# Attention, then two expert layers: 576-query score units in PSUM pairs, one product bank, a tied TensorE order

## The chip, the cores and the metric

One core of one Trainium2 chip. The metric is the device time of one execution in microseconds. The engines are named as in the profile: PE (TensorE, with PEld for its weight loads), DVE (VectorE), ACT (ScalarE), POOL (GpSimd) and SP (SyncE, which here only issues DMAs).

## The reference

```
q_pool = q.reshape(B, H, S // 2, 2, D).mean(axis=3)           # B, H, S, D = 4, 8, 1152, 64
scores = scale * q_pool @ k^T                                 # 576 x 1152 for each of 32 heads
attn   = exp(scores - max); attn /= sum(attn) + 1e-9
x      = attn @ v                                             # heads side by side: 2304 x 512
x      = moe(x)        # top-1 of 8 experts, 512 -> 1024 -> 512, times the gate
out    = (h * cos(h)) @ w_out,  h = x @ w_in                  # 512 -> 2048 -> 512
```

All inputs are float32. The kernel keeps float32 accuracy by splitting operands into a high and a low part (fp32r for scores, f16 for weights and values) and adding the products.

## The kernel before

The program has three stages: attention (32 heads, the first 616 us of the profiled execution), the experts, and the cosine layer. The change touches attention alone, and the DMAs that fill `y_d` with zeros while attention runs.

For each head i, in this order:

- `load` (L111 to L123) fetches k, q, v. The q pairs are added, k and q are split (ACT `q_high`, `k_high`; DVE or POOL `q_low`, `k_low`), transposed on PE into PSUM tiles `pk`, `pq`, copied out by ACT as `k1`, `q1`, and rearranged in SBUF by DMAs (`k2`, `q2`). `v` is scaled by a power of two and split into `va` (high by POOL L177, low by DVE L182).
- `scores` and `row_max` (L247, L262): PE makes 128 x 384 score tiles `pm`; DVE reduces each to row maxima `mm`. 12 tiles for an odd head, 15 for an even head, which does the last 64 queries of its odd neighbour along with its own. `max_all` (L268) reduces them to `mx`, and `max_row` (L277) has SP write the negated maxima into a row of `q2` by small DMAs (4 for a head, 2 more for the shared rest).
- `weight_scores` (L287, L288): the scores again, transposed (128 keys by queries), with the maximum subtracted by the extra row of `q2`. Nine groups c of 128 keys, each in two halves j of 288 queries; a half `pst` takes one of three PSUM banks. `weight_exp` (L296): ACT takes the exponential of each half into the SBUF tile `pf`, 128 x 576.
- `weight_high` and `weight_low` (L308 to L318): `ph` is `pf` cast to f16, `pl` the rest. The nine casts are spread as 6 on ACT, 1 on DVE and 2 on POOL, the nine subtractions as 2 on DVE (c = 4 and 7) and 7 on POOL.
- `values` (L335 to L337): for each of five query tiles a run of 27 matmuls (9 groups by three products) into a PSUM bank of its own, `po`; ACT copies it to `pe` (L341). `normalise` (L359 to L362) on DVE divides by the row sums and writes the head's columns of `xf` and `xs`.

The heads are software-pipelined: while PE makes weight scores of head i it also makes maxima of head i+1, products of head i-1, and transposes of heads i+2 and later. The order comes from `plan`: each step is given a time from the table `G` in units where a head takes T = 12.8; steps are issued sorted by that time, and a scheduler that simulates the program then orders each engine's instructions, so that two steps that are near in the plan may change places or interleave. PSUM has 8 banks: 3 for `pst` (pool `ps2`), 3 for `pm` and small things (`psm`), 2 for `pk`, `pq` and `po` (`ps1`).

`Routing.plan` adds, after each batch of 8 heads, transposes of x, gate logits, ranks, and on POOL 4 or 5 indirect DMAs (`scatter`, L483). `Routing.zeros` (L505 to L510) makes SP issue 18 DMAs of 256 KB of zeros into `y_d`, all at one place of the plan, after head 2.

Of the kernel before, what the change touches and what calls it, by code (L numbers as in the profile page):

```python
# [8 lines left out]
F32 = mybir.dt.float32  # L9
# [20 lines left out]
    kh=3.8, kl=5.8, qp=4.5, qh=5.3, ql=6.3, vm=5.15, va=6.0, vs=8.0, vh=10.3,  # L30
    vl=10.5, qt=1.05, qc=0.6, q2=0.9, q1=2.95, k0=2.25, kg=1.7, kc=0.05, kd=1.7,
    o0=0.1, mo=0.78, m=0.8, mr=0.3, ma=0.0, md=0.4, w=3.35, e=1.7, h=0.8,
    l=0.55, v=3.2, vc=2.8, vt=0.3, vx=0.3, n=1.1,
)
HI_ACT = (0, 2, 4, 5, 6, 8)
HI_DVE = (3,)
LO_DVE = (4, 7)
K_COPY_DVE = ()
QEARLY = (2, 3)
# [4 lines left out]
class Attention:  # L44
# [15 lines left out]
    def __init__(self, tc, ctx, pools, q, k, v, ident, xpool):  # L60
# [12 lines left out]
        self.k2, self.q1, self.q2, self.va, self.mm, self.qr, self.pe = [], [], [], [], [], [], []  # L73
# [7 lines left out]
        const(self.pe, (cp,) * 2, "pe", [5, 66])  # L81
# [25 lines left out]
    def set_pe(self, i):  # L107
        self.nc.gpsimd.memset(self.pe[i], 1.0)


    def load(self, i):  # L111
        nc = self.nc
        b, h = divmod(i, H)
        s = self.st[i] = {}
        qr = self.qr[i % 2]
        s["kr"] = kr = self.p1.tile([P, NK, D], F32, tag="kr", name=f"kr_{i}")
        s["vr"] = vr = self.p1.tile([P, NK, D], F32, tag="vr", name=f"vr_{i}")
# [5 lines left out]
        nc.sync.dma_start(vr, self.v[b, h].rearrange("(p c) d -> p c d", p=P))  # L123
# [12 lines left out]
    def q_low(self, i):  # L136
        s = self.st[i]
        eng = self.nc.gpsimd if i in QEARLY else self.nc.vector
# [47 lines left out]
    def k_transpose(self, i, g):  # L186
        nc, s = self.nc, self.st[i]
        ps = s["pk", g] = self.ps1.tile([P, 512], F32R, tag="ps1", name=f"pk_{i}_{g}")
# [3 lines left out]
    def k_copy(self, i, g):  # L192
# [4 lines left out]
        if g in K_COPY_DVE:  # L197
            nc.vector.tensor_copy(o, s["pk", g][:, :384])
        else:
            nc.scalar.copy(o, s["pk", g][:, :384])  # L200
# [11 lines left out]
    def q_transpose(self, i, part):  # L212
        nc, s = self.nc, self.st[i]
        pool, tag = ((self.ps1, "ps1"), (self.psm, "psm"))[part]
# [32 lines left out]
    def scores(self, i, ci, g):  # L247
        nc = self.nc
        ps = self.st[i]["pm", ci, g] = self.psm.tile([P, 512], F32, tag="psm", name=f"pm_{i}_{ci}_{g}")
        ks = slice(g * 384, (g + 1) * 384)  # L250
        if ci < 4:
            q0 = self.q_cols(i, 0)[0].start + ci * P
            nc.tensor.matmul(  # L253
                ps[:, :384], self.st[i]["q1"][:, q0 : q0 + P], self.st[i]["k1"][:, ks], start=True, stop=True
            )
            return
        for h in (i, i + 1):
            q = self.q1[h % 4][:, 512:] if h == i else self.q1[h % 4][:, :P]
# [11 lines left out]
    def max_row(self, i, part):  # L270
        mx = self.mx[i % 4].bitcast(F32)
        for h, o, c in [(i, 0, c) for c in range(4)] if part == 0 else [(i, 0, 4), (i + 1, 64, 4)]:
# [4 lines left out]
            self.nc.sync.dma_start(row, mx[o : o + n, c : c + 1])  # L277


    def weight_scores(self, i, c, j):  # L280
        nc, s = self.nc, self.st[i]
        if (c, j) == (0, 0):
            s["ph"] = self.pw.tile([P, NK, SQ], F16, tag="ph", name=f"ph_{i}")
            s["pl"] = self.pw.tile([P, NK, SQ], F16, tag="pl", name=f"pl_{i}")
        ps = s["pst", c, j] = self.ps2.tile([P, 512], F32, tag="ps2", name=f"pst_{i}_{c}_{j}")
        ks, o = slice(c * P, (c + 1) * P), slice(j * 288, (j + 1) * 288)
        nc.tensor.matmul(ps[:, :288], s["k1"][:, ks], s["q1"][:, o], start=True, stop=False)  # L287
        nc.tensor.matmul(  # L288
            ps[:, :288], self.k2[i % 3][: D + 2, ks], self.q2[i % 4][: D + 2, o], start=False, stop=True
        )  # L290

    def weight_exp(self, i, c, j):
        nc, s = self.nc, self.st[i]
        if j == 0:
            s["pf", c] = self.p3.tile([P, SQ], F32, tag="pf", name=f"pf_{i}_{c}", bufs=4)
        nc.scalar.activation(  # L296
            s["pf", c][:, j * 288 : (j + 1) * 288], s["pst", c, j][:, :288], AF.Exp, scale=0.0625
        )

    def weight_high(self, i, c):  # L300
        nc, s = self.nc, self.st[i]
        ph, pf = s["ph"][:, c, :], s["pf", c]
        if i == B * H - 1:
            hi_act, hi_dve = (0, 2, 4, 6, 8), (1, 3, 5, 7)
        else:
            hi_act, hi_dve = HI_ACT, HI_DVE
        if c in hi_act:
            nc.scalar.copy(ph, pf)  # L308
        elif c in hi_dve:
            nc.vector.tensor_copy(ph, pf)  # L310
        else:
            nc.gpsimd.tensor_scalar(ph, pf, 1.0, 0.0, op0=ALU.mult, op1=ALU.add)

    def weight_low(self, i, c):
        nc, s = self.nc, self.st[i]
        lo_dve = (0, 2, 3, 5, 6, 8) if i == B * H - 1 else LO_DVE
        eng = nc.vector if c in lo_dve else nc.gpsimd
        low = eng.tensor_sub(s["pl"][:, c, :], s["pf", c], s["ph"][:, c, :])  # L318
        if c not in lo_dve:
            self.low = getattr(low, "ins", low)  # L320
# [5 lines left out]
    def values(self, i, ci, third):  # L326
# [3 lines left out]
        if third == 0:  # L330
            s["po", ci] = self.ps1.tile([P, 512], F32, tag="ps1", name=f"po_{i}_{ci}")
        po, va = s["po", ci][self.rows(i, ci), :], s["va"]
        for c in range(3 * third, 3 * third + 3):
# [12 lines left out]
    def normalise(self, i):  # L346
# [8 lines left out]
        pe = self.pe[i % 2]  # L355
# [3 lines left out]
        nc.vector.tensor_scalar(r, pe[:, :, D], PSC * 1e-9, s["iv"], op0=ALU.add, op1=ALU.mult)  # L359
        nc.vector.reciprocal(r, r)  # L360
        nc.vector.tensor_mul(full[:, :, cols], pe[:, :4, :D], r[:, :4].unsqueeze(2).to_broadcast([P, 4, D]))
        nc.vector.tensor_scalar_mul(self.xs[b // 2 * 9 + 4][half, cols], pe[half, 4, :D], r[half, 4:5])  # L362

    def plan(self, at, n=B * H):

        for t, f, m in (
            (-1.95, self.set_qr, 2), (-0.9, self.set_q, 4), (-0.3, self.set_q2, 4), (0.0, self.set_k, 3),
            (0.3, self.set_v, 5), (1.0, self.set_pe, 2),
# [3 lines left out]
        for i in range(n):  # L372
# [34 lines left out]
            for c in range(NK):  # L407
                z9 = w + c * T / NK
                for j in range(2):
                    a(z9 + T / 18 * j, self.weight_scores, c, j)  # L410
                    a(z9 + T / 18 * j + G["e"], self.weight_exp, c, j)
                a(z9 + T / 18 + G["e"] + G["h"], self.weight_high, c)
                a(z9 + T / 18 + G["e"] + G["h"] + G["l"], self.weight_low, c)
# [1023 lines left out]
```

## Time and profile before

| | |
|---|---|
| three runs, us | 1355.69, 1356.85, 1363.11 (median 1356.85) |
| the profiled execution | 1359.03 us; its span, first to last instruction, 1357.4 us |
| granted TensorE clock, mean over the span | 0.957 |
| busy share of the span | PE 91%, DVE 75%, ACT 54%, POOL 48% |
| attention, first exponential to last | 39.4 us to 609.8 us |

The profile is of one execution. "Busy" of an engine is the time covered by its instructions. PE's matmuls overlap (a product matmul lasts 0.19 us, and the next starts 0.03 us after it), so its busy time is more than the time that it needs; the distance from one start to the next says what a matmul costs. A clock of 1.00 is 2.4 GHz and 0.50 is 1.2 GHz.

### The profile page before, as it was taken

Reading aid. Unit: us, or ns where it says so; the run is one execution under the profiler, and the core shown is the slowest. Engines: PE = TensorE matmul, PEld = TensorE weight load, DVE = VectorE, ACT = ScalarE, POOL = GpSimd, SP = SyncE. Lnnn points to the kernel's source line nnn. Section 1 sums busy time; section 2 is a strip of 40 time slices with the busy share of each in tenths; the row PEclk is TensorE's granted clock in tenths of the full one; section 3 lists DMA queues with packets and bytes.
Section 4 is the critical chain, followed back from the end, with each engine's and each line's share of the span. In section 5 each row is a group of like instructions: output and inputs, shape, how many; then the busy total and the mean of one; then the engine's idle time right before and its main releaser. Section 6 shows DMA issues by size and latency. Waiting matters only on the chain. (4 is left out here: it accounts for less than half of the span.)

```text
span 1357.4 us, 26889 instructions
## 1 busy us (share of the span) xinstructions
PE 1237.3 (91%) x10190; PEld 1049.8 (77%) x10190; DVE 1021.3 (75%) x1921; ACT 728.0 (54%) x1631; POOL 654.9 (48%) x585
## 2 busy tenths in 40 slices
PE   5897999999889997999699898987998999999996
PEld 4786887888778786878588788866887888888885
DVE  6896888997879878886368788977765667667664
ACT  4685886788758775882265555664322223222232
POOL 6796888798779877751244435526002002010010
PEclk8798998999989998999799999999999999999998
DMA  8349344343433332324588879975002001000000
GB/s 182 88 111 191 83 98 87 100 102 82 108 80 89 81 99 47 99 64 91 119 248 300 258 239 288 318 245 186 1 0 65 1 0 63 0 32 15 0 32 16
DMA packets 117691, 146.20 MB, mean 108 GB/s; under 512 B 34864, under 2 KB 73904, under 8 KB 117552
## 3 DMA queue, kind: packets, MB, share of 16 engines
q1 hardware_dynamic: 104176, 114.97, 32.0%
q0 software_dynamic: 5600, 15.25, 3.6%
q10 hardware_dynamic: 7776, 14.17, 3.2%
q8 instruction: 82, 1.34, 0.5%
q14 instruction: 57, 0.47, 0.1%
HBM read 97.57 MB, written 28.43 MB: 93 GB/s over the span
## 5 line engine op out<-in xcount | busy, mean ns | idle before, releaser
L318 POOL TENSOR_TENSOR pl<-pf,ph 128x576 f16<-128x576 f32 x220 | 306.1, 1404 | 54.8 <-ACT ph L308 38.0
L262 DVE TENSOR_REDUCE mm<-pm 128x1 f32<-128x384 f32 x432 | 224.7, 546 | 54.4 <-PE pm L253 40.0
L296 ACT ACTIVATE pf<-pst 128x288 f32<-128x288 f32 x576 | 222.1, 421 | 81.1 <-PE pst L288 52.6
L287 PE MATMUL pst<-q,k 128*128 128x288 f32 x576 | 199.1, 351 | 1.8 <-ACT pf L296 1.6
L483 POOL DMA_INDIRECT out_dram<-os,token x18 | 18.2, 1013 | 354.5 <-ACT os L1200 186.9
L288 PE MATMUL pst<-q,k 66*128 66x288 f32 x576 | 173.9, 308 | 14.9 <-DMA q<-mx 14.9
L337 PE MATMUL po<-va,pl 128*128 128x66 f16 (+1 forms) x1440 | 176.8, 198 | 6.3 <-DVE pl L318 5.1
L335 PE MATMUL po<-va,ph 128*128 128x66 f16 (+1 forms) x1440 | 176.1, 198 | 0.3 <-ACT pe L341 0.3
L336 PE MATMUL po<-va,ph 128*128 128x64 f16 (+1 forms) x1440 | 175.1, 196 | 0.0
L1171 ACT ACTIVATE a<-a,hpi 128x512 f32<-128x512 f32 (+1 forms) x80 | 54.5, 681 | 201.9 <-DVE a L1170 192.3
L253 PE MATMUL pm<-k,q 128*128 128x384 f32 x384 | 148.8, 411 | 14.9 <-DVE mm L262 12.6
L335 PEld LDWEIGHTS <-ph 128*128 128x128 f16 (+1 forms) x1440 | 136.4, 103 | 23.7 <-issue 10.6
L337 PEld LDWEIGHTS <-pl 128*128 128x128 f16 (+1 forms) x1440 | 137.6, 102 | 21.2 <-DVE pl L318 8.4
L336 PEld LDWEIGHTS <-ph 128*128 128x128 f16 (+1 forms) x1440 | 138.3, 102 | 6.9 <-issue 2.7
L308 ACT CAST ph<-pf 128x576 f16<-128x576 f32 x191 | 129.8, 682 | 1.2
L288 PEld LDWEIGHTS pst<-q,k 66*128 66x128 f32 x576 | 114.7, 200 | 15.7 <-DMA q<-mx 15.7
L1161 PE MATMUL ch<-zh,w1h_m 128*128 128x512 f32 (+1 forms) x320 | 119.5, 374 | 3.5 <-ACTq L1386 3.5
L287 PEld LDWEIGHTS pst<-q,k 128*128 128x128 f32 x576 | 114.4, 199 | 6.4 <-ACT pf L296 3.6
L1161 PE MATMUL ch<-zl,w1h_m 128*128 128x512 f32 (+1 forms) x320 | 119.3, 373 | 0.0
L1161 PE MATMUL ch<-zh,w1l_m 128*128 128x512 f32 (+1 forms) x320 | 119.1, 372 | 0.0
L1185 PE MATMUL po<-w2h_m,gh 128*128 128x512 f32 x288 | 114.1, 396 | 0.0
L1185 PE MATMUL po<-w2l_m,gh 128*128 128x512 f32 x288 | 114.1, 396 | 0.0
(262 smaller groups left out, 3273.2 us busy)
## 6 DMA issues: line engine op xcount, KB each, us to landing
w1r_e<-in_moe_w_dram SPq DMA_DIRECT2D x32, 512.0 KB, 5.7
w2r_e<-in_moe_w_dram SPq DMA_DIRECT2D x32, 512.0 KB, 5.2
kr<-in_k_dram SPq DMA_DIRECT2D x32, 288.0 KB, 3.4
vr<-in_v_dram SPq DMA_DIRECT2D x32, 288.0 KB, 3.2
k<-k SPq DMA_DIRECT2D x32, 288.0 KB, 3.4
q<-q SPq DMA_DIRECT2D x60, 144.0 KB, 2.8
qr<-in_q_dram SPq DMA_DIRECT2D x32, 256.0 KB, 4.1
raw<-in_moe_w_in_dram SPq DMA_DIRECT2D x16, 512.0 KB, 6.0
```

Source lines behind the costliest of these rows:

```text
L253: nc.tensor.matmul(ps[:, :384], self.st[i]["q1"][:, q0 : q0 + P], self.st[i]["k1"][:, ks], start=True, stop=True)
L262: self.nc.vector.tensor_reduce(self.mm[i % 2][:, ci, g : g + 1], self.st[i]["pm", ci, g][:, :384], axis=AX.X, op=ALU.max)
L287: nc.tensor.matmul(ps[:, :288], s["k1"][:, ks], s["q1"][:, o], start=True, stop=False)
L288: nc.tensor.matmul(ps[:, :288], self.k2[i % 3][: D + 2, ks], self.q2[i % 4][: D + 2, o], start=False, stop=True)
L296: nc.scalar.activation(s["pf", c][:, j * 288 : (j + 1) * 288], s["pst", c, j][:, :288], AF.Exp, scale=0.0625)
L308: nc.scalar.copy(ph, pf)
L318: low = eng.tensor_sub(s["pl"][:, c, :], s["pf", c], s["ph"][:, c, :])
L335: nc.tensor.matmul(po[:, :66], hi, va[:, c, D:130], start=(c == 0), stop=False)
L336: nc.tensor.matmul(po[:, :D], hi, va[:, c, :D], start=False, stop=False)
L337: self.product = nc.tensor.matmul(po[:, :66], lo, va[:, c, D:130], start=False, stop=(c == NK - 1))
L1161: nc.tensor.matmul(ph[:, :n], wt[:, c, fs], z[:, c, :n], start=(k == 0), stop=(k == 3 * NDC - 1))
L1185: nc.tensor.matmul(po[j], g[:, ts], wt[:, f % FC, :], start=(f == 0 and k == 0), stop=(f == NFC2 - 1 and k == 2))
```

## The change

- A unit of weight scores is now 128 keys by all 576 queries: four matmuls into the two banks of one PSUM tile (288 queries in each), and one exponential over both. The pool `ps2` holds two such pairs (four banks), `psm` three banks, which now also serve `pk` and `pq`, and `pso` one bank. 
- In units 1, 4 and 7 (all nine in the last head) the exponential is written back to PSUM; ACT casts it from there (`ph`), DVE subtracts from there (`pl`), and only then is the pair free. The other six units go through `pf` as before, cast by ACT and subtracted by POOL. DVE and POOL cast no more weights.
- The five product runs of a head lie side by side in the one bank of `pso`, and DVE normalises from PSUM. The five ACT copies to `pe` go; the sums' addition and reciprocal become two DVE instructions each.
- From the plan's time 2T to the last unit's start every PE instruction is tied behind the one that the plan issues before it, so that the scheduler can't change PE's order.
- `q_low` of head 2 and later is on POOL (before: heads 2 and 3 alone). The v loads get a third buffer.
- The 18 zero DMAs are issued one after each head from head 3 on, behind the SP queue's latest row of maxima.
- Most numbers of `G` differ.

```
 G = dict(
-    kh=3.8, kl=5.8, qp=4.5, qh=5.3, ql=6.3, vm=5.15, va=6.0, vs=8.0, vh=10.3,
+    kh=4.31, kl=5.82, qp=4.44, qh=4.91, ql=7.56, vm=4.58, va=5.24, vs=8.03, vh=10.3, vl=10.82, qt=-1.58, qc=0.42,
...
-HI_ACT = (0, 2, 4, 5, 6, 8)
-HI_DVE = (3,)
-LO_DVE = (4, 7)
+INPLACE = (1, 4, 7)
+PF = 4
+BANKS = (2, 3, 1)
+TIE = 2
...
-        self.ps2 = ctx.enter_context(tc.tile_pool(name="at_ps2", bufs=3, space=PSUM))
-        self.psm = ctx.enter_context(tc.tile_pool(name="at_psm", bufs=3, space=PSUM))
-        self.ps1 = ctx.enter_context(tc.tile_pool(name="at_ps1", bufs=2, space=PSUM))
+        self.ps2, self.psm, self.pso = (
+            ctx.enter_context(tc.tile_pool(name=f"at_{k}", bufs=n, space=PSUM))
+            for k, n in zip(("ps2", "psm", "pso"), BANKS)
+        )
...
+        ps = self.ps2.tile([P, 1024], F32, tag="ps2", name=f"pst_{i}_{u}")
+        ps = s["pst", u] = ps.rearrange("p (two q) -> p two q", q=512)[:, :, :QH]
+        ks = slice(u * P, (u + 1) * P)
+        for n in range(2):
+            q = slice(n * QH, (n + 1) * QH)
+            o = ps[:, n, :]
+            nc.tensor.matmul(o, s["k1"][:, ks], s["q1"][:, q], start=True, stop=False)
+            nc.tensor.matmul(o, self.k2[i % 3][: D + 2, ks], self.q2[i % 4][: D + 2, q], start=False, stop=True)
+
+    def weight_exp(self, i, u):
...
+        if u in self.inplace(i):
+            nc.scalar.activation(pst, pst, AF.Exp, scale=0.0625)
+            return
+        pf = self.p3.tile([P, SQ], F32, tag="pf", name=f"pf_{i}_{u}", bufs=PF)
+        s["pf", u] = pf.rearrange("p (two q) -> p two q", q=QH)
+        nc.scalar.activation(s["pf", u], pst, AF.Exp, scale=0.0625)
+    def inplace(self, i):
+        return range(NK) if i == B * H - 1 else INPLACE
+    def split(self, i, u):
...
+        nc.scalar.copy(ph, pst)
+        nc.vector.tensor_sub(pl, pst, ph)
...
-        if third == 0:
-            s["po", ci] = self.ps1.tile([P, 512], F32, tag="ps1", name=f"po_{i}_{ci}")
+        if ci == 0:
+            s["po"] = self.pso.tile([P, 5, 66], F32, tag="po", name=f"po_{i}")
...
-    def values_copy(self, i, ci):
-        o = self.rows(i, ci)
-        self.nc.scalar.copy(self.pe[i % 2][o, ci, :], self.st[i]["po", ci][o, :66])
...
+        for q, c in ((slice(0, P), slice(0, 4)), (half, slice(4, 5))):
+            nc.vector.tensor_scalar(r[q, c], po[q, c, D], PSC * 1e-9, s["iv"][q], op0=ALU.add, op1=ALU.mult)
+            nc.vector.reciprocal(r[q, c], r[q, c])
+        nc.vector.tensor_mul(full[:, :, cols], po[:, :4, :D], r[:, :4].unsqueeze(2).to_broadcast([P, 4, D]))
...
+    def tie(self, made):
+        order = mybir.DependencyInfo(mybir.DependencyClass.NoSync, mybir.DependencyReason.DATA)
+        for i in made:
+            if i.engine == mybir.EngineType.PE:
+                if self.last is not None:
+                    self.tc.add_manual_dep(i, self.last.name, order)
+                self.last = i
...
+    def zero(self, y_d, r, row):
+        with self.tc.issue_after(row()):
+            self.nc.sync.dma_start(y_d[r : r + P, :DM], self.z)
...
+        for n, r in enumerate(range(YROW[NU], YROW[NU] + NX * U, P)):
+            plan(att.end(ZAT + 1 + n) + 0.1, rt.zero, y_d, r, lambda: att.row)
```

Three places show how instructions move. Names carry head and unit: `pst_15_1` is unit 1 of head 15 (before: `pst_15_1_0` its first half).

ACT, from the first exponential of head 15 on. Before:

```order
L296 ACTIVATE pf_15_0_5708<-pst_15_0_0_5670 128x288
L296 ACTIVATE pf_15_0_5708<-pst_15_0_1_5681 128x288
L200 COPY k1_17_5673<-pk_17_2_5769 128x384
L144 CAST ks_19_6068<-kr_19_5970 128x9x64
L296 ACTIVATE pf_15_1_5753<-pst_15_1_0_5689 128x288
L602 COPY xt_1_4419<-px20_1_5830 128x512
L308 CAST ph_15_5668<-pf_15_0_5708 128x576
L602 COPY xt_1_4419<-px21_1_5853 128x128
L296 ACTIVATE pf_15_1_5753<-pst_15_1_1_5724 128x288
L296 ACTIVATE pf_15_2_5805<-pst_15_2_0_5747 128x288
```

Now:

```order
L302 ACTIVATE pf_15_0_5297<-pst_15_0_5281 128x576
L197 COPY k1_17_5240<-pk_17_2_5293 128x384
L144 CAST ks_19_5662<-kr_19_5571 128x9x64
L317 CAST ph_15_5279<-pf_15_0_5297 128x576
L298 ACTIVATE pst_15_1_5301<-pst_15_1_5301 128x2x288
L302 ACTIVATE pf_15_2_5379<-pst_15_2_5331 128x576
L311 CAST ph_15_5279<-pst_15_1_5301 128x576
L317 CAST ph_15_5279<-pf_15_2_5379 128x576
L621 COPY xt_1_4062<-px20_1_5373 128x512
L302 ACTIVATE pf_15_3_5398<-pst_15_3_5382 128x576
```

Unit 1's cast, on which its pair of banks waits, stands behind the exponential of unit 2; in 27 of the first 31 heads an exponential stands there, at unit 4 in 17 of them and at unit 7 in 13.

PE, around units 1 and 2 of head 15, now (before, the halves of a unit stood apart, with pieces of product runs between them, such as the three rows that are shown last):

```order
L291 MATMUL pst_15_1_5301<-q1_3_120,k1_15_4578 128x288
L292 MATMUL pst_15_1_5301<-q2_3_127,k2_0_121 128x288
L251 MATMUL pm_16_2_0_5308<-k1_16_4919,q1_0_117 128x384
L251 MATMUL pm_16_2_1_5329<-k1_16_4919,q1_0_117 128x384
L291 MATMUL pst_15_2_5331<-q1_3_120,k1_15_4578 128x288
L292 MATMUL pst_15_2_5331<-q2_3_127,k2_0_121 128x288
L162 MATMUL ar_18_5336<-ident_60,am_18_5317 128x128
```

```order
L288 MATMUL pst_15_1_0_5689<-q2_3_129,k2_0_123 128x288
L337 LDWEIGHTS pl_14_5323
L337 MATMUL po_14_0_5755<-va_4_134,pl_14_5323 128x66
L335 LDWEIGHTS ph_14_5322
L335 MATMUL po_14_0_5755<-va_4_134,ph_14_5322 128x66
```

Each unit's first two matmuls are followed by the two for its other bank (same names). Behind the last row shown of the order now come the 27 products of `po_14`'s first run, in one piece, one tile of maxima, and unit 3.

DVE, from the subtraction of unit 1 of head 15 on, now:

```order
L312 TENSOR_TENSOR pl_15_5280<-pst_15_1_5301,ph_15_5279 128x576
L172 RECIPROCAL iv_18_5442<-pw_18_5438 128x1
L261 TENSOR_REDUCE mm_0_111<-pm_16_3_0_5390 128x1
L261 TENSOR_REDUCE mm_0_111<-pm_16_3_1_5396 128x1
L182 SCALAR_TENSOR_TENSOR va_3_131<-vr_18_5221,iv_18_5442,va_3_131 128x9x64
L261 TENSOR_REDUCE mm_0_111<-pm_16_3_2_5445 128x1
L265 TENSOR_REDUCE mx_0_113<-mm_0_111 128x4
L261 TENSOR_REDUCE mm_0_111<-pm_16_4_0_5453 128x1
L312 TENSOR_TENSOR pl_15_5280<-pst_15_4_5433,ph_15_5279 128x576
```

The subtraction reads the pair of unit 1 in PSUM (`pst`) and its f16 cast in SBUF; the maxima of head 16 that follow it come from PE rows behind unit 3. `mx_0` of head 16, from which its first unit gets the maxima, is made between units 4 and 5 of head 15; before, it was made when unit 0 of head 15 began.

## Rows read from the trace of the kernel before

**Rows 1.** Stretches (us), ACT's exponentials alone (L296): busy us, their number, clock, DMA share.

```profile
102.40:129.80 27.40, 6.84 (x19) 0.89 0.98 194
214.80:240.70 25.90, 6.86 (x19) 0.80 0.41 56
240.70:357.90 117.20, 48.68 (x127) 0.99 0.40 101
357.90:386.30 28.40, 6.98 (x19) 0.88 0.24 53
501.80:528.20 26.40, 6.90 (x18) 0.87 0.18 30
sum 570.40, ACT 221.68; mean ACT 24.63
```

**Rows 2.** SP's timeline, and PE's longest wait from 100 to 135 us.

```profile
109.81 8.34 SPq L510 DMA_DIRECT2D y_d<-z  x7
118.25 5.54 SPq L277 DMA_DIRECT2D q<-mx  x4
PE pst L288 <- DMA q<-mx: 9.3, 1, 9.3
```

**Rows 3.** Timelines of DVE and POOL from 223 us: start us, us, engine, line.

```profile
225.22 4.37 DVE L318 TENSOR_TENSOR pl<-pf,ph 128x576 f16<-128x576 f32 x1
226.33 1.41 POOL L149 TENSOR_TENSOR ks<-kr,ks 128x576 fp32r<-128x576 f32 x1
```

**Rows 4.** One stretch: busy us of PE, PEld, DVE, ACT, POOL (number), clock, DMA.

```profile
240.70:357.90 117.20, 109.78 (x1397) 95.02 (x1396) 100.38 (x201) 93.88 (x258) 100.26 (x82) 0.99 0.40 101
375.00:380.00 5.00, 0.44 (x14) 0.33 (x11) 1.15 (x3) 0.14 (x1) 4.76 (x5) 0.95 0.18 30
380.00:385.00 5.00, 4.90 (x34) 4.55 (x35) 2.84 (x6) 1.15 (x3) 2.85 (x4) 0.50 0.13 30
```

**Rows 5.** Groups by line, 240.7 to 357.9 us: busy, mean ns | idle before.

```profile
L262 DVE TENSOR_REDUCE mm<-pm 128x1 f32<-128x384 f32 x88 | 46.1, 547 | 10.6 <-PE pm L253 7.0 <-PE pm L259 3.3
L318 DVE TENSOR_TENSOR pl<-pf,ph 128x576 f16<-128x576 f32 x14 | 13.8, 988 | 0.6 <-ACT ph L308 0.5
L318 POOL TENSOR_TENSOR pl<-pf,ph 128x576 f16<-128x576 f32 x48 | 68.1, 1432 | 7.6 <-ACT ph L308 4.9 <-DVE ph L310 2.6
L312 POOL TENSOR_SCALAR ph<-pf 128x576 f16<-128x576 f32 x14 | 10.8, 768 | 0.0
L308 ACT CAST ph<-pf 128x576 f16<-128x576 f32 x41 | 28.0, 686 | 0.2
L341 ACT COPY pe<-po 128x66 f32<-128x66 f32 x28 | 5.7, 220 | 4.4 <-PE po L337 4.4
L200 ACT CAST k<-pk 128x384 fp32r<-128x384 f32 x20 | 9.9, 497 | 2.4 <-PE pk L190 2.4
```

**Rows 6.** By line: xcount, duration ns min/median/max, first and last start us.

```profile
L318 DVE TENSOR_TENSOR pl<-pf,ph x68: 737/968/4369, 48.5 to 611.5; 128x576 f16<-128x576 f32 x68
L1069 DVE TENSOR_TENSOR xl_e<-pt_e,xh_e x18: 677/681/692, 668.7 to 883.4; 128x512 fp32r<-128x512 f32 x18
```

**Rows 7.** Timelines of ACT (three exponentials back to back) and PE, at full clock.

```profile
221.05 1.02 ACT L296 ACTIVATE pf<-pst 128x288 f32<-128x288 f32 x3
279.82 0.29 PE L287 MATMUL pst<-q,k 128*128 128x288 f32 x1
280.36 0.21 PE L335 MATMUL po<-va,ph 128*128 128x66 f16 x1
281.19 0.51 PE L218 MATMUL pq<-idr,qs 128*128 128x128 f32 x4
284.00 0.42 PE L253 MATMUL pm<-k,q 128*128 128x384 f32 x1
284.25 0.37 PE L190 MATMUL pk<-idr,ks 128*128 128x128 f32 x3
```

**Rows 8.** DMAs issued from 205 to 245 us: issues, KB each, median us to landing.

```profile
q<-mx SPq DMA_DIRECT2D x8, 0.5 KB, 3.8
```

More of the change, by code (lines that the diff above doesn't have):

```diff
@@ L187, in k_transpose @@
         nc, s = self.nc, self.st[i]
-        ps = s["pk", g] = self.ps1.tile([P, 512], F32R, tag="ps1", name=f"pk_{i}_{g}")
+        ps = s["pk", g] = self.psm.tile([P, 512], F32R, tag="psm", name=f"pk_{i}_{g}")
         for j in range(3):
@@ L196, in k_copy @@
         o = s["k1"][:, g * 384 : (g + 1) * 384]
[L197 to L200, printed above, removed]
+        nc.scalar.copy(o, s["pk", g][:, :384])
     def k_second(self, i):
@@ L276, in max_row, with piece, weight_scores @@
             row = self.q2[h % 4][D : D + 1, q0 : q0 + n].bitcast(F32)
-            self.nc.sync.dma_start(row, mx[o : o + n, c : c + 1])
-    def weight_scores(self, i, c, j):
+            self.row = getattr(d := self.nc.sync.dma_start(row, mx[o : o + n, c : c + 1]), "ins", d)
+    def piece(self, t, u):
+        return t[:, u, :].rearrange("p (two q) -> p two q", q=QH)
+    def weight_scores(self, i, u):
         nc, s = self.nc, self.st[i]
-        if (c, j) == (0, 0):
+        if u == 0:
             s["ph"] = self.pw.tile([P, NK, SQ], F16, tag="ph", name=f"ph_{i}")
@@ L329, in values @@
         n = P if ci < 4 else 64
-        if third == 0:
-            s["po", ci] = self.ps1.tile([P, 512], F32, tag="ps1", name=f"po_{i}_{ci}")
-        po, va = s["po", ci][self.rows(i, ci), :], s["va"]
-        for c in range(3 * third, 3 * third + 3):
+        if ci == 0:
+            s["po"] = self.pso.tile([P, 5, 66], F32, tag="po", name=f"po_{i}")
+        po, va = s["po"][self.rows(i, ci), ci, :], s["va"]
+        for c in range(NK):
             hi, lo = s["ph"][:, c, q0 : q0 + n], s["pl"][:, c, q0 : q0 + n]
@@ L406, in plan, with __init__ @@
             w = T + G["w"]
[L407 to L413, printed above, removed]
+            for u in range(NK):
+                z9 = w + u * T / NK
+                a(z9, self.weight_scores, u)
+                a(z9 + G["e"], self.weight_exp, u)
+                if u in self.inplace(i):
+                    a(z9 + G["e"] + G["h"], self.split, u)
+                else:
+                    a(z9 + G["e"] + G["h"], self.weight_high, u)
+                    a(z9 + G["e"] + G["h"] + G["l"], self.weight_low, u)
             v = w + T + G["v"]
             for ci in range(5):
-                for third in range(3):
-                    a(v + ci * G["vc"] + third * G["vt"], self.values, ci, third)
-                a(v + ci * G["vc"] + 3 * G["vt"] + G["vx"], self.values_copy, ci)
+                a(v + ci * G["vc"], self.values, ci)
             a(v + 5 * G["vc"] + G["n"], self.normalise)
     def end(self, i):
-        return i * T + 2 * T + G["w"] + G["v"] + 5 * G["vc"] + G["n"]
+        return i * T + 2 * T + G["w"] + G["v"] + 5 * G["vc"] + G["n"] + G["em"]
 class Plan:
-    def __init__(self):
+    def __init__(self, tc, start, end):
+        self.tc = tc
+        self.span = start, end
         self.steps = []
+        self.last = None
     def __call__(self, t, f, *args):
@@ L435, in run @@
     def run(self):
-        for _, _, f, args in sorted(self.steps, key=lambda s: s[:2]):
+        for t, _, f, args in sorted(self.steps, key=lambda s: s[:2]):
+            traced = self.tc.nc.cur_bb.bb.instructions
+            n = len(traced)
             f(*args)
+            if self.span[0] <= t < self.span[1]:
+                self.tie(traced[n:])
+    def tie(self, made):
[5 more added lines that the diff above has]
+                self.last = i
 NE, DF, DF2 = 8, 1024, 2048
```

106 lines of the change are left out of this document (40 added, 66 removed).

## The prediction

> **What bounds it now.** I read the stretches first, then what each slow one waits for, then the engines' shares and single durations. The 32 heads take 570.4 us [rows 1], 17.8 each, and not evenly. Eighteen exponentials are a head: 240.7 to 357.9 holds 127, so seven heads in 117.2 us, 16.7 each. Four heads take 27.4, 25.9, 28.4 and 26.4 us, in sum 108.1; the other 28 take 462.3, or 16.5 each. In an ordinary head DVE and POOL are each busy 100 of 117 us, 14.3 a head, ACT 13.4 [rows 4]. PE's 109.8 overstates its need. From start to start, 27 products cost 0.83 us, four weight-score matmuls 0.54, a tile of maxima 0.18 to 0.25, three k transposes about 0.21 [rows 7]. So a head needs five runs, 4.15; nine units, 4.86; 15 tiles at 0.2, 3.0; three triples, 0.63; the q transposes, about 0.6. That is 13.25, and with an estimate of 0.65 for routing's share **13.9 us**. Hence 2.6 us of an ordinary head is PE waiting, and the slow heads are waits alone.
>
> The slow heads have two causes. At 102.4 us SP is taken by zero writes: seven take 8.3 us to issue, the maxima's rows come behind them, and PE waits 9.3 us for one [rows 2]. The other three follow a batch of eight heads, where POOL's index writes come on top. There one DVE subtraction took 4.37 us while POOL ran its own without a break [rows 3]; alone it takes 0.74 [rows 6]. PE then idles and works on at half clock: 0.44 us of matmuls in 375 to 380, then 0.50 granted (1.2 GHz) to 385 [rows 4].
>
> **What the change does to the loads,** per ordinary head.
> - DVE: the two subtractions at 0.99 [rows 5] become three that read PSUM. The nearest row, an equal one of 512 columns from PSUM, lasts 0.68 and never over 0.69 [rows 6]; I take 0.75 for 576. That adds 0.25, but the f16 cast and the q subtraction go, and normalising reads PSUM, which adds two or three small instructions and removes waits of the kind in [rows 3]. Bounds: 14.3 (nothing gained) and 11.8 (normalising and the subtractions wait for POOL no more); I take 12.5. The Trainium skill says in "SBUF — State Buffer", "Who interferes with whom", that VectorE waits for GpSimd only with two inputs from SBUF or in its two-port modes; by that DVE would be at 11.8, and the sum below would stay, since DVE is not its longest term. The 18 subtractions from PSUM in [rows 6] agree; for normalising from PSUM the trace has no row.
> - POOL: one of seven subtractions (1.43) and two casts (0.77 each) go [rows 5]; the q subtraction comes, at under 1.4, since it has 320 columns where 1.43 is for 576. 14.3 becomes 12.7.
> - ACT: 18 exponentials cost 6.1 back to back (three in 1.02) [rows 7]. A unit of 576 lies between one half (0.34) and a cast of the same size alone (0.69) [rows 5]; less the overlap of some 0.1 I take 0.56, nine are 5.0. Three casts more, 3 x 0.58 = 1.7; the copies of `po` go, (5.7 + 1.1) / 7 = 1.0 at most. 13.4 becomes about 13.2.
> - PE: the same matmuls, in fewer pieces; 13.9 stays.
>
> So PE, at 13.9, is the longest and the others have a microsecond or so to spare. What decides is how long PE waits in its fixed order.
>
> **The new wait.** Only two pairs of banks exist, so unit u+2 needs the pair of u. For six units it is free after the exponential. For units 1, 4 and 7 it is free after exponential, cast and DVE subtraction. At unit 1 ACT's order is the exponential of 0, a k copy, the k cast, cast 0, exponentials 1 and 2, cast 1: 0.56 + 0.38 + 0.57 + 0.57 + 0.56 + 0.56 + 0.67 = 3.9 us (the casts by their 0.69 and the k copy by its 0.50, each less 0.12 of overlap; the last in full) [rows 5]. It begins some 0.75 after unit 0's first matmul, and DVE's 0.75 follows: unit 3 can start at 5.4. PE's own work from unit 0 to unit 3 is three units, 1.62, five tiles, 1.0, a triple, 0.21, a run, 0.83, in all 3.7 us. **PE waits 1.7 us**, and all that stands behind unit 3 waits with it. Bounds: 0, if ACT is early (each of its pieces was priced with none of its idle time used), and 3, if two reductions of 0.55 stand before the subtraction. Unit 4 has the exponential of 5 before its cast in 17 of 31 heads, which I price at 0.8, so 0.4 on average; unit 7's cast is followed by enough PE work. Sum: 13.9 + 1.7 + 0.4 = 16.0, less 0.4 of routing work, which falls into the waits: **15.6 us**. The old wait of 2.6 becomes 1.7.
>
> The maxima come later than before: `mx` of an even head is now made four units before its first use, where it was nine. Four units of a head of 15.6 are 6.9 us; mm 0.55, mx, four issues and a landing of 3.8 [rows 8] are about 6.5. I cost it at nothing; the cover is 0.4 us thick, and behind a 256 KB write it may be gone in some heads.
>
> The five runs in one bank: products of the next head must wait for normalising. By the order three units and a few tiles, over 2.5 us of PE work, lie between the last run and the next head's first, and DVE needs six short instructions and three reductions, about 2.7. It costs nothing to 0.5; I take nothing.
>
> **The slow heads.** The zero writes come one a head, 0.5 us of SP each, behind rows of maxima. The 10.9 us of the head at 102.4 go but for 1. For the three batch heads, 25.9 + 28.4 + 26.4 - 3 x 16.5 = 31.2 of excess: the index writes stay, DVE's subtraction no longer stands in POOL's way. Bounds 0 and 31; I leave half, 15.6.
>
> **Sum.** 32 x 15.6 = 499.2, plus 1 and 15.6, is 515.8 against 570.4: 54.6 less. The stages behind attention are the same and start so much earlier. The profiled execution took 1359.0 us, 2.2 above the median of the runs: 1304.4, and **1302 us** at the median.
>
> **Rivals.**
> - PE finds its pairs free (unit 1's exponential and cast come early, since ACT has slack): 13.9 to 14.1 a head, 32 x 14.0 + 16.6 = 464.6, time 1251. For it: ACT's 13.2 leaves room. Against: the order puts exponential 2 before cast 1 in 27 of 31 heads. Chance 0.14.
> - Ordinary heads stay at 16.5, as the tied order can't step aside where the old one did; only the slow heads shorten, by 9.9 + 15.6 = 25.5: 1331. For it: the waits of 2.1 that I find are near the old 2.6. Chance 0.20.
> - **Slower**: the pairs come back late at all three in-place units, not at one. The place is DVE's queue: the subtraction behind two reductions (2 x 0.55) and cast behind exponential. It decides when a head's waits pass 570.4 / 32 - 0.5 - 13.9 = 3.4 us, or 1.1 a unit. At unit 1's 1.7 for all three it is 13.9 + 5.1 = 19.0 a head: 624.6 in all, 1411 us. For it: two pairs only, and PE tied. Against: units 4 and 7 have a product run and 1.5 us of other work behind them. Chance 0.12.
> - Also slower: PE's waits drop its clock. After 375 to 380 it ran 5 us at 0.50, so lost 2.5 [rows 4]; once a head, that is 15.6 + 2.5 = 18.1, and 32 x 18.1 + 16.6 = 595.8: 1382. Against it, the stretch of seven heads has waits of 2.6 a head and a clock of 0.99 [rows 4]; chance 0.04. A section of the Trainium skill speaks for it ("TensorE: Matmul & The Clock Gate", on a second failure mode, depth-cycling of the PSUM queue): a PE that idles briefly between groups while it goes round its PSUM banks can swing between the two clocks. By that rule the time would be the 1382; the trace of before, with a round of three banks, does not bear it out.
>
> **Chances and range.** My forecast has 0.50, with 1270 to 1330 as its own range (15.6 a head give or take 0.5, and the batch heads' bounds). Half a percent, 6.8 us, is about what a measurement can tell from no change. Faster by more: 0.50 + 0.14 + 0.16 of the second rival = 0.80. Slower: 0.14 of the last two. Within: 0.06, from the ends of those. Range 1246 to 1350: it leaves out the slower rivals, 0.16, and thin ends of the others.
>
> **What would show it.** Right: about 15.6 us from head to head; at units 3 of most heads a wait of 1 to 2 us of PE for DVE's subtraction (L312) and few others; that subtraction near 0.75 and not stretched; DVE and POOL near 12.6 a head; no stretch of 27 us with the zero writes. Wrong: PE's longest wait is for the rows of maxima (then the four units are too short), or for normalising, or PE's clock falls in ordinary heads; or a head under 14.2.

## The result and the profile after

The changed kernel takes **1316.33 us** (median of four runs, 1315.65 to 1321.14) against 1359.55 for the kernel before beside it: ratio 0.969, 95% interval 0.965 to 0.973. Measured once more, on another chip and in other runs, the ratio was 0.967 (0.963 to 0.972). The forecast was 1302 with a range of 1246 to 1350: 54.6 us off, where 43.2 came. The profiled execution's span is 1314.1 us, its mean clock 0.971.

Attention, first exponential to last, went from 570.4 us [rows 1] to 569.4 - 42.4 = 527.0, so the whole gain lies there. Eight heads at a time (ACT alone: busy us, number, clock, DMA share, GB/s):

```profile
42.40:163.00 120.60, 108.79 (x205) 1.00 0.45 112
163.00:301.40 138.40, 111.01 (x211) 0.96 0.50 112
301.40:440.00 138.60, 110.56 (x207) 0.96 0.49 106
440.00:569.40 129.40, 106.02 (x194) 1.00 0.36 82
```

The same eights of the kernel before took 141.0, 143.5, 142.4 and 143.5 us. The first eight gain 20 (the storm of zero writes was there, [rows 2]), the last 14; the middle ones, in which index writes and routing stand, gain 4 to 5 each. In the first eight, heads take 13.8 to 14.0 and 15.5 to 15.6 us in turn (even, odd); the eighth takes 18.3, as six routing matmuls of 0.43 us stand in it. So a head without routing takes 14.75 on average. Longer heads, most of them at the ends of batches (the longest 20.3, 20.5, 21.3, 21.3 and 23.7 us), make attention 55 us longer than 32 x 14.75. The forecast's own split, 28 ordinary heads and four slow ones, is taken up below.

PE's clock rose as well. The whole of attention in the kernel before, in the changed kernel without its tie (the first experiment below), and with the change (busy us of PE, PEld, DVE, ACT, POOL; clock, DMA share, GB/s):

```profile
39.40:609.80 570.40, 526.01 (x6409) 450.41 (x6409) 479.13 (x961) 428.16 (x1158) 457.39 (x384) 0.95 0.39 95
41.20:609.70 568.50, 531.66 (x6415) 445.09 (x6415) 415.31 (x996) 440.19 (x814) 364.37 (x316) 0.97 0.40 96
42.40:569.40 527.00, 492.63 (x6413) 429.41 (x6412) 415.28 (x995) 436.38 (x815) 364.12 (x316) 0.98 0.45 103
```

These traces show two levels only, 1.00 and 0.50, so that the means stand for 60, 36 and 20 us at 0.50 (24 in the second trace of the change).

What PE waited for, 60 to 560 us (total, times, longest):

```profile
PE pm L251 <- DVE mm L261: 6.3, 11, 1.4
PE pst L292 <- DMA q<-mx: 5.7, 4, 3.9
PE pst L291 <- DVE pl L312: 4.1, 5, 1.4
PE po L338 <- issue: 3.1, 4, 1.4
PE pst L291 <- DVE r L359: 1.5, 7, 0.2
```

The third line is the wait on which the forecast was built, 1.7 us a head: it cost 4.1 us in all. Groups of DVE and POOL in the same stretch (busy, mean ns | idle before), to set beside [rows 5, 6]:

```profile
L312 DVE TENSOR_TENSOR pl<-pst,ph 128x576 f16<-128x576 f32 x92 | 68.5, 745 | 4.5 <-ACT ph L311 3.6 <-ACT pf L302 0.5
L360 DVE TENSOR_TENSOR xf<-po,r 128x256 f32<-128x256 f32 x30 | 12.5, 415 | 0.3
L321 POOL TENSOR_TENSOR pl<-pf,ph 128x576 f16<-128x576 f32 x180 | 234.6, 1305 | 95.2 <-ACT ph L317 80.0 <-PE pst L292 9.7 <-POOL pl L321 1.8
```

The subtraction from PSUM lasts 745 ns and never over 759, where the one from SBUF had a mean of 988 and a worst case of 4369. POOL now idles behind ACT's casts.

### The profile page after: what moved, and what is told of

Same layout as the page of the kernel before. It is cut to its first block, busy times and chain, and to the rows that moved or that the text cites. A ratio compares the mean times of both kernels' runs of the same rounds, so it can differ in the third digit from the quotient of the medians.

```text
span 1314.1 us, 26532 instructions
## 1 busy us (share of the span) xinstructions
PE 1207.9 (92%) x10190; PEld 1033.9 (79%) x10190; DVE 954.2 (73%) x1956; ACT 733.8 (56%) x1280; POOL 562.7 (43%) x515
## 5 line engine op out<-in xcount | busy, mean ns | idle before, releaser
L321 POOL TENSOR_TENSOR pl<-pf,ph 128x576 f16<-128x576 f32 x186 | 242.3, 1304 | 100.1 <-ACT ph L317 84.8
L261 DVE TENSOR_REDUCE mm<-pm 128x1 f32<-128x384 f32 x432 | 229.2, 549 | 76.0 <-PE pm L251 58.5
L291 PE MATMUL pst<-q,k 128*128 128x288 f32 x576 | 177.2, 321 | 10.1 <-DVE pl L312 4.7
L292 PE MATMUL pst<-q,k 66*128 66x288 f32 x576 | 166.0, 302 | 6.0 <-DMA q<-mx 5.7
L337 PE MATMUL po<-va,ph 128*128 128x66 f16 (+1 forms) x1440 | 154.7, 195 | 2.9 <-issue 1.9
L338 PE MATMUL po<-va,ph 128*128 128x64 f16 (+1 forms) x1440 | 153.1, 194 | 3.1 <-issue 3.1
L339 PE MATMUL po<-va,pl 128*128 128x66 f16 (+1 forms) x1440 | 152.6, 196 | 1.1 <-DVE pl L312 1.1
L251 PE MATMUL pm<-k,q 128*128 128x384 f32 x384 | 144.6, 396 | 9.6 <-DVE mm L261 8.0
L337 PEld LDWEIGHTS <-ph 128*128 128x128 f16 (+1 forms) x1440 | 134.4, 102 | 15.3 <-issue 3.9
L302 ACT ACTIVATE pf<-pst 128x576 f32<-128x576 f32 x186 | 122.4, 658 | 30.5 <-PE pst L292 23.1
L338 PEld LDWEIGHTS <-ph 128*128 128x128 f16 (+1 forms) x1440 | 136.1, 101 | 2.8 <-issue 2.6
L292 PEld LDWEIGHTS pst<-q,k 66*128 66x128 f32 x576 | 111.7, 194 | 7.7 <-issue 5.4
```

The lines of the kernel that those rows point to most:

```text
L251: nc.tensor.matmul(ps[:, o], self.st[i]["q1"][:, q0 : q0 + P], self.st[i]["k1"][:, ks], start=True, stop=True)
L261: self.nc.vector.tensor_reduce(mm[:, ci, g : g + 1], pm[:, :MK], axis=AX.X, op=ALU.max)
L291: nc.tensor.matmul(o, s["k1"][:, ks], s["q1"][:, q], start=True, stop=False)
L292: nc.tensor.matmul(o, self.k2[i % 3][: D + 2, ks], self.q2[i % 4][: D + 2, q], start=False, stop=True)
L302: nc.scalar.activation(s["pf", u], pst, AF.Exp, scale=0.0625)
L321: low = self.nc.gpsimd.tensor_sub(self.piece(s["pl"], u), s["pf", u], self.piece(s["ph"], u))
```

## The experiments

Each is named with its edit; ratios are to the kernel before, in runs on the same chip. Where attention's length is told, it is first exponential to last in the profile (570.4 before, 527.0 with the change, 522.0 in a second trace of it).

**The tie.** First theory: the gain comes from lighter DVE and POOL queues.

```
-        plan = Plan(tc, TIE * T, B * H * T + G["w"])
+        plan = Plan(tc, 1e9, 1e9)
```

> The changed kernel, but no PE instruction is tied to the plan's order; the scheduler may reorder PE as in the kernel before. Theory (the gain of 43 us comes from lighter DVE and POOL queues and from the spread zero writes, the tie only keeps an order that the scheduler would nearly choose): within 10 us of the changed kernel's 1316, so 1306 to 1326. Rival (the order is what gains: without the tie PE's waits of the kernel before come back): 1340 or more. Second rival (the tie holds PE behind late routing steps at the ends of batches): 1295 to 1306, with the heads of 20 to 24 us at 197, 317 and 338 shortened.

Measured: 1360.8 us, ratio 1.0013 (0.9988 to 1.0038), attention 568.5. The first rival's time holds, and my theory falls: without the tie, lighter queues (DVE 415 us busy in attention, as with the tie) and spread zero writes gain nothing in the sum, though PE idles less (37 us of attention for 44) and runs less at half clock. The rival's reason falls too: the old waits don't come back. From 60 to 160 us PE of the untied kernel has one listed wait; this is the whole list, and the busy line of the first seven heads (PE, PEld, DVE, ACT, POOL):

```profile
PE pk L190 <- DVE mm L261: 0.4, 1, 0.4
41.20:150.80 109.60, 107.32 (x1301) 92.00 (x1300) 85.27 (x204) 94.60 (x177) 80.49 (x71) 1.00 0.46 111
```

PE is busy 107.3 of 109.6 us at full clock and still needs 15.7 a head, where the changed kernel's first seven take 14.6. The same matmuls cost more in another order. PE's timeline, of the untied kernel:

```profile
77.06 0.19 PE L338 MATMUL po<-va,ph 128*128 128x64 f16 x1
77.09 0.42 PE L251 MATMUL pm<-k,q 128*128 128x384 f32 x1
77.35 0.20 PE L339 MATMUL po<-va,pl 128*128 128x66 f16 x1
```

and of the changed one:

```profile
77.66 0.30 PE L292 MATMUL pst<-q,k 66*128 66x288 f32 x1
77.79 0.34 PE L251 MATMUL pm<-k,q 128*128 128x384 f32 x1
77.97 0.30 PE L291 MATMUL pst<-q,k 128*128 128x288 f32 x1
```

Behind a product a tile of maxima holds PE 0.26 us; behind another score matmul 0.18. These are also the medians over attention, at full clock and with no idle time, in the kernel before, untied, with the change and in the next three kernels; a weight-score matmul holds PE 0.22 and 0.14. So each return from products to scores costs 0.08. The weight loads suggest why (PEld of the changed kernel: busy, mean ns):

```profile
L251 PEld LDWEIGHTS pm<-k,q 128*128 128x128 f32 x351 | 65.8, 192 | 18.2 <-DVE mm L261 11.7 <-issue 1.7 <-DVE pw L170 0.6
L338 PEld LDWEIGHTS <-ph 128*128 128x128 f16 x1089 | 101.0, 97 | 2.8 <-issue 2.6
```

A score's load lasts 192 ns, and a product leaves 30 to hide it behind. The Trainium skill says in "TensorE: Matmul & The Clock Gate", "Back-to-back issue gap", that the spacing of matmuls is set by the weight load and the matmul together; these rows agree. By the written-out orders, PE goes into a piece of products 414 times in the attention of the kernel before, 447 untied, 157 with the tie. The plan of the kernel before itself sets a run of 27 in three pieces, 0.3 apart (`vt`). The change's plan sets it as one step, which the list of the change does not say; without the tie the scheduler still cuts it into 2.8 pieces, and the tie keeps it whole. That is the second theory, and the next three kernels test it.

**Pieces, with the tie on.** `values` gets its thirds back, `for third in range(3): a(v + ci * G["vc"] + 0.65 * third, self.values, ci, third)`.

> The changed kernel, tied as it is, but each product run is put into the plan in three pieces 0.65 apart, so that PE goes into a piece 370 times in attention instead of 157 (untied 447, the kernel before 414). In the untied run's timeline the first score matmul behind a product piece lasts 0.42 us and holds PE 0.26, where one behind another score matmul lasts 0.34 and holds it 0.18. Theory (the tie gains because it keeps the runs whole, 0.08 us for each piece saved): 213 more pieces cost 17 us, so 1328 to 1340. Rival (pieces are free; what the tie gains is waits that a fixed order avoids): 1312 to 1322.

Measured: 1348.75 us, ratio 0.9969 (0.9945 to 0.9992), attention 557.3. 213 more pieces cost 30 to 35 us of attention. Not all of it is pieces: a wait that the changed kernel hardly has is listed,

```profile
PE po L337 <- DVE xs L361: 13.4, 14, 1.5
```

the next head's first product behind normalising, since each run now ends later. Without it 17 to 22 us remain, **0.08 to 0.10 a piece**. That subtraction is rough, since other waits got shorter (PE idles 39 us in all, for 34 with the change); the table under the next heading gives 18.5 us for the pieces in another way, 0.09 each. The theory of whole runs holds; the time misses the expected range by the bank's wait and by 12 us more at half clock (33 for 20), which I had not priced.

**The tie alone.** The kernel before with the change's `Plan`, over the same stretch; then also `vt=0.3, vx=0.3` set to `vt=0.0, vx=0.9`, so that the plan has a run's thirds at one time.

> The kernel before with the tie alone, over the same stretch; its plan puts runs in three pieces, 411 in all against 414. Theory of whole runs: nothing is saved in pieces, so no gain from them, and a plan that was not made for a fixed order waits in more places: 1350 to 1385. Rival (a fixed order by itself gains, as untying the changed kernel cost 44 us): 1335 or less.

> The same with the three pieces of a run put at one time of the plan (161 pieces); the copy of the result stays where it was. Theory of whole runs: 250 pieces x 0.08 = 20 us less than the tied kernel before with 411 pieces, give or take 6. Rival (pieces are free): within 5 us of it.

Measured: 1404.9 us (ratio 1.037, 1.033 to 1.041), then 1387.4 (1.026, 1.023 to 1.030); attention 626.1 and 597.8. A fixed order by itself loses 3.7%, more than either range: PE's transposes of x wait 21.2 us for DVE's reductions in 13 places, its tiles of maxima 17.7, and its clock is lower (0.91 over attention). Whole runs give back 17.5 us by the times and 28 by the profiles for 250 pieces, 0.07 to 0.11 each. So neither the tie nor whole runs carry over alone. The changed kernel has other plan times, loads and banks besides; which of these makes the fixed order pay is not shown.

The start times in the traces part the pieces from the rest. "Need" counts every matmul of attention at the median distance to the next one that its kind has at full clock with no idle time, matmuls behind a product and behind others apart; "idle" is time with no matmul running:

| attention, us | before | untied | thirds | change | before, tied | before, tied, whole |
|---|---|---|---|---|---|---|
| length | 570.4 | 568.5 | 557.3 | 527.0 | 626.1 | 597.8 |
| pieces | 414 | 447 | 370 | 157 | 411 | 161 |
| PE's need | 459 | 461 | 459 | 441 | 459 | 437 |
| PE idle | 44 | 37 | 39 | 34 | 76 | 75 |
| at half clock | 60 | 36 | 33 | 20 | 107 | 90 |

Need follows the pieces: it falls by 18 to 23 us for 213 to 290 pieces, 0.07 to 0.09 each. Of the 43 us between before and change it is 19. The rest is PE's clock and waits: 10 us less idle, and by the spacings at either clock (0.24 for 0.14 of a weight-score matmul) the 40 us less at half clock are worth about 14. Of the 41.5 between untied and change 20 are need, about 7 idle time and half clock; some 14 are short stalls between matmuls that no list shows, and their cause stays open.

**The split of DVE and POOL.** In one kernel units 1, 4 and 7 go through `pf` (the pair is free after the exponential, DVE reads SBUF twice; the last head stays); in the other `q_low` is on DVE again, with PE's order unchanged.

```
-        if u in self.inplace(i):
+        if i == B * H - 1:
...
-        eng = self.nc.gpsimd if i >= FIRST else self.nc.vector
+        eng = self.nc.gpsimd if i in (2, 3) else self.nc.vector
```

> The changed kernel, but units 1, 4 and 7 go through the SBUF tile pf like the others (last head as it was): their pair is free after the exponential, and DVE's three subtractions a head read SBUF twice. Theory (DVE and POOL stand in each other's way only with two SBUF inputs; the pair's wait is small, 4.1 us in 32 heads): the subtraction goes from 0.745 us to about 0.95, POOL's from 1.30 to about 1.4; time 1318 to 1330. Rival (the prediction's wait for the pair costs 1 to 2 us a head, and goes): 1280 to 1305.

> The changed kernel, but the low part of q is subtracted on DVE as before for heads 4 and later; PE's order is the same. DVE gets 28 x 0.75 to 0.9 us, POOL loses 28 x 0.9 to 1.1. Theory (after the change neither DVE, busy 415 of 527 us, nor POOL, 364, is what a head waits for): within 4 us of 1316. Rival (DVE's queue is still what PE waits for at maxima and pairs): half a microsecond or more a head, 1330 or more.

Measured: 1321.95 us (0.9755, 0.9733 to 0.9776) and 1327.0 (0.9789, 0.9761 to 0.9817). With the tie on both parts pay, 6 and 11 us by the times, 9 and 13 by the ratios; without the tie neither was taken back by itself. The first time is in its theory's range; the second is under its rival's 1330. DVE's subtraction and PE's longest lists of waits, the first two lines of the SBUF kernel, the last of `q_low`:

```profile
L313 DVE TENSOR_TENSOR pl<-pf,ph 128x576 f16<-128x576 f32 x89 | 108.8, 1223 | 3.8 <-ACT ph L312 3.6
PE pm L251 <- DVE mm L261: 17.4, 31, 3.2
PE pk L190 <- DVE mm L261: 18.5, 15, 2.8
```

From SBUF the subtraction takes 1223 ns, not 745, nor the 0.95 that I expected, and PE waits 17.4 us for reductions behind it (6.3 before). With `q_low` DVE is busy 433 of 540 us, and yet its queue holds PE up 18.5 us in 15 places: as I read it, an engine at 80% is late now and then, and a tied PE can't step aside. My theory of no effect fell. With the pairs freed early PE's listed waits for them are gone (4.1 us with the change), but the slower subtraction came with it, so that the run gives no price for the pair's wait alone; it is small.

**The zero writes.** All 18 at one place again in the changed kernel (`plan(att.end(ZAT) + 0.2, rt.zero, ...)`); and spread in the kernel before, with the change's `zero`.

> The changed kernel, but all 18 zero writes are issued at one place behind head 2, as before. Theory (the writes at one place block SP's queue ahead of the rows of maxima, some 10 us of PE wait once): 1324 to 1330, with one head of 22 to 26 us near 100 us. Rival (the changed kernel has its rows of maxima out elsewhere, so that the block hits nothing): within 3 us of 1316.

> The kernel before with its 18 zero writes issued one after each head as in the change, nothing else. Theory (the 9.3 us wait for the rows of maxima at 119 us goes and nothing takes its place): 1344 to 1350. Rival (the time is given back at the ends of batches, as where the changed kernel with all writes at one place lost only 6 us for a head that was 13 us longer): 1350 to 1358.

Measured: 1322.1 us (0.9764, 0.9721 to 0.9807) and 1352.45 (1.0004, 0.9984 to 1.0024). The storm is real where it stands: once more a head of 27.7 us, with this wait in the changed kernel's version:

```profile
PE pst L292 <- DMA q<-mx: 16.6, 5, 13.2
```

But heads at the ends of batches were shorter there (15.3 and 14.9 for 20.5 and 23.7), so the loss is 6 us by the times and 10 by the ratios, not 13, and the time lies between the two ranges. In the kernel before, the head at 102 us went from 27.4 to 15.4, and the one after the first batch from 25.9 to 34.8: PE waited 8.0 us for one row of maxima, whose four issues took SP 5.66 us beside the index writes. Alone the spread gained nothing, as the rival said.

```profile
PE pst L288 <- DMA q<-mx: 8.0, 1, 8.0
221.25 5.66 SPq L277 DMA_DIRECT2D q<-mx  x4
```

**The index writes.** In the changed kernel's slow head at 197 us PE stands in the middle of a run, with no semaphore to wait for, while POOL goes on:

```profile
203.97 0.19 PE L337 MATMUL po<-va,ph 128*128 128x66 f16 x1
205.61 0.19 PE L338 MATMUL po<-va,ph 128*128 128x64 f16 x1 [1.45 <-issue]
206.37 0.19 PE L337 MATMUL po<-va,ph 128*128 128x66 f16 x1 [0.54 <-issue]
207.81 0.23 PE L338 MATMUL po<-va,ph 128*128 128x64 f16 x1 [0.53 <-issue]
201.62 0.98 POOL L499 DMA_INDIRECT idx_d<-toki,dest  x1 [0.16 <-issue]
206.04 1.01 POOL L499 DMA_INDIRECT idx_d<-toki,dest  x1 [0.17 <-issue]
```

DVE and ACT wait 5.0 and 5.1 us there, and PE then runs from 207.4 to 214.3 at 0.50 (1.2 GHz). Of the 51 loads of 16 KB of instructions in attention on queue q8, 46 took 0.88 to 1.57 us; the other five, 3.0 to 4.1, began within 6.1 us of such a write. The next two kernels change `step = 1.0 if late else SSTEP`: to `T` for batches 0 and 1; then to `(T, T, 4.0, 1.0)[batch]`. The third is the changed kernel beside the second.

> The changed kernel, but the index writes of batches 0 and 1 come one a head (a step of 12.8 in the plan instead of 2.5); PE's order is the same. In the changed kernel's trace all engines but POOL stand for up to 4 us beside these writes, rows of maxima land late, and the heads at 197 and 338 us take 20.5 and 23.7 us. Theory (four or five writes close together slow all other DMAs, instruction loads and rows of maxima among them; alone each is covered): those two heads fall below 18, and the time to 1302 to 1311. Rival (each write costs its share wherever it stands): within 4 us of 1316, the loss spread over ten heads.

> The changed kernel with the index writes of batches 0 and 1 one a head and those of batch 2 at a step of 4.0 (2.5 before). In the profile with the first two spread, attention was 522.3 us from first exponential to last against 527.0, and the heads at 197 and 338 took 14.7 and 13.9 instead of 20.5 and 23.7, but the heads of the third batch stayed at 18.4, 20.9, 17.8 with two slow instruction loads (3.2 and 3.6 us). Theory (writes close together slow the other DMAs): the third batch's heads lose 2 to 4 us more; attention 518 to 521, time 6 to 10 us below the changed kernel on the same chip. Rival (the time is paid elsewhere, as the median of the first trial hardly told it apart): within 3 us of the changed kernel on the same chip.

> The changed kernel itself, beside the run with spread index writes on the same chip. Both theories: 0.965 to 0.973 of the kernel before, as measured first; by the theory of the index writes a second trace again has a head of over 20 us where the writes of batches 0 and 1 stand, with an instruction load of PE of 3 us or more beside it.

Measured: 1311.85 us (0.9683, 0.9660 to 0.9705), 1309.7 (0.9683, 0.9650 to 0.9716) and 1310.35 (0.9674, 0.9633 to 0.9716). The two heads do shrink, from 20.5 and 23.7 to 14.7 and 13.9 (14.2 in the second). But in the repeated change they took 17.1 and 18.3 of themselves, while with spread writes the heads at their new places went from 16.7 and 16.6 to 18.6 and 18.7. Attention is 522.3, 523.4 and 522.0. PE's waits for late rows, of the repeated change and then of the second spread:

```profile
PE pst L292 <- DMA q<-mx: 8.7, 6, 3.8
PE pst L292 <- DMA q<-mx: 1.7, 2, 1.1
```

Nor did the repeat have the head of over 20 us that the theory asked for. One load of 3.8 us stands beside its first batch's writes and none of over 2 beside the second's; and a single write at 197.5 us, with nothing near it, had one of 3.3 in the first spread. The wait for rows goes and the time does not, so that spreading gains nothing (the first time lies just outside both ranges, the second in its rival's). That a write costs its share wherever it stands fits this. What one costs when it is not there at all was not tried, because experts read its result. That the slow loads cause PE's stop at 204 is likely by their place, not shown.

**Fewer returns still.** Runs 0 and 1, and 2 and 3, back to back: `(0, 0, 2, 2, 4)[ci] * G["vc"]`.

> The changed kernel, but product runs 0 and 1, and 2 and 3, of a head stand back to back in the plan: PE enters products 98 times instead of 157. Theory (0.08 us for each return to scores): 59 x 0.08 = 4.7 us less, 1308 to 1314. Rival (1.7 us of products in one piece starves ACT's exponentials, and pairs of banks come late behind them): 1320 or more.

Measured: 1323.25 us (0.9761, 0.9718 to 0.9805), attention 534.4. The rival's time holds. PE's need, counted as in the table, does fall by 5 us, to 436, as the theory has it. Part of the loss is one late row of maxima, `PE pst L292 <- DMA q<-mx` 6.1 us, beside index writes; in 60 to 190 ACT waited 6.4 us for transposed q (2.5 with the change as it is) and 4.0 for score units to take into `pf` (2.4). So here the trade of pieces against supply seems to end at one run, by a small margin: the two intervals, 0.965 to 0.973 and 0.972 to 0.981, touch. No kernel here beats the change clearly.

## Why the prediction came out as it did

- **The loads: about right, and not what gained.** DVE came to 415 / 32 = 13.0 us a head (12.5 said), ACT 13.6 (13.2), POOL 11.4 (12.7). The Trainium skill's rule in "SBUF — State Buffer", "Who interferes with whom", agrees with the traces: DVE's subtraction takes 745 ns from PSUM and 1223 from SBUF, and normalising from PSUM, for which I had no row, takes 415 ns instead of 794 (the kernel before, 60 to 560 us, below). But untied, the same loads gave a ratio of 1.0013.

```profile
L361 DVE TENSOR_TENSOR xf<-pe,r 128x256 f32<-128x256 f32 x27 | 21.4, 794 | 0.1
```

- **PE's need: the step that failed.** "PE: the same matmuls, in fewer pieces; 13.9 stays." I saw the fewer pieces and gave them no price, though [rows 7] held it: the tile at 284.00 stands right behind a product, and the "0.18 to 0.25" that I took as a spread is the two cases. 257 fewer pieces are worth 19 us by the table, 0.6 a head, not quite half of the 43 measured; PE's need was 14.4 a head before and is 13.8 now. Nor was the 2.6 us of an ordinary head waiting. This is the whole list of PE's waits in the seven heads from 240.7 to 357.9 of the kernel before, 7.3 us or 1.0 a head:

```profile
PE pm L253 <- DVE mm L262: 3.2, 4, 2.0
PE px L596 <- DVE xs L362: 2.5, 2, 1.3
PE po L337 <- DVE pl L318: 1.3, 3, 0.5
PE ar L162 <- DVE mm L262: 0.3, 1, 0.3
```

  I also had not asked what the tie gains, and read it only as a cause of waits; and the sum took PE's clock into account only inside the slow heads, where half of those 60 us at 0.50 lie.
- **The new wait: a wrong premise.** "Only two pairs of banks exist, so unit u+2 needs the pair of u." ACT, PE and DVE show otherwise, at the head of 72 us:

```profile
74.64 0.65 ACT L302 ACTIVATE pf<-pst 128x576 f32<-128x576 f32 x1
75.34 0.41 PE L291 MATMUL pst<-q,k 128*128 128x288 f32 x1
75.98 0.75 DVE L312 TENSOR_TENSOR pl<-pst,ph 128x576 f16<-128x576 f32 x1
76.26 0.68 ACT L302 ACTIVATE pf<-pst 128x576 f32<-128x576 f32 x1
```

  The exponential of unit 2 ends at 75.29, PE begins unit 3 at 75.34 and its exponential starts at 76.26, while DVE still reads unit 1's pair until 76.73. Unit 3 therefore stands in unit 2's pair; in 24 of the 29 heads in which I could pair the rows, unit 3's exponential starts before unit 1's subtraction ends. The in-place pair is held aside while the other pair serves units 2 and 3. For heads without routing (14.75) the rival "PE finds its pairs free", 14.0 a head, was about as near as my 15.6.
- **Maxima, bank, zeros.** PE waited 5.7 us for late rows in four places (8.7 in six in the second trace), the longest beside index writes: a thin cover, as said, costing little. Normalising held PE 1.5 us in all, by its reciprocals ahead of score units, inside "0 to 0.5" a head. The zero writes were to give 9.9; the head did shrink from 27.4 to 13.8, but by the two kernels the writes are worth 0 to 10, since batch ends take it back.
- **The slow heads: near in the sum, by luck.** By the forecast's own split, the three batch heads took 20.5, 23.7 and 19.3, in sum 63.5, where 46.8 + 15.6 = 62.4 were forecast. The head of the zero writes took 13.8 for 16.6. The other 28 took 449.7, or 16.06 each for 15.6: the 11 us that the total was off are there, within the half microsecond a head that I allowed. But the 28 are not alike. Heads without routing took 14.75, so that 32 of them at 15.6 are 27 too long; over 32 x 14.75 stand 55 us (50 in the second trace) in place of my 16.6, so 38 more. Some of that is work that I had spread over all heads as routing's 0.65 (six matmuls of 0.43 in the head at 144.7); some is stops beside index writes and half clock after them (0.83 granted over 197 to 217). So the total is near because two errors leaned against each other, and the excess of the batch heads, half of its bounds, was a guess: in the second trace the same three take 17.1, 18.3 and 19.5.
- **The slower rivals.** Pairs late at three units: excluded by the 4.1 us of waits for the subtraction. Clock falling in every head: it is 1.00 over the first eight. The Trainium skill's second failure mode ("TensorE: Matmul & The Clock Gate", on psum-queue depth-cycling), by which it would have swung, is not borne out with two pairs either.

## What to carry to other kernels

A long matmul right behind a short one held PE 0.08 us longer here, so count the returns from short to long matmuls in PE's order before calling its time fixed. A scheduler that fills PE's gaps may pay for them in cut runs. A fixed order is no gain by itself (the same tie: 44 us of gain in one kernel, 50 of loss in the other), and where it gains, small loads on the other queues start to count. Divide a measured gain into matmul spacing, idle time and clock before naming its cause. Two buffers don't mean strict turns: see which one the third user takes.

## What the hardware showed that I had not expected

- A 128x384 score tile holds PE 0.26 us behind a product and 0.18 behind another score.
- Index writes of 128 values of 4 bytes by POOL come with slow loads elsewhere: PE's 16 KB of instructions take 3.0 to 4.1 us instead of about 1.1, four rows of maxima take SP 5.66 us to issue, where they take 2.44 at 60 and 76 us in the kernel before, and PE stops inside a run without a semaphore. That the writes cause the rest is not shown.
- How long single heads at batch ends take differs between executions of one program (23.7 and 18.3 us for the same head), though the totals of ten runs of it lie between 1300.9 and 1321.1; so a head is no evidence where a time is wanted.
